# Two tiny transfers more, transposes moved between value rows, and some weight loads split or merged in a multimodal attention block

## The chip, the core and the metric

The kernel runs on one core of one Trainium2 chip. Its time is the device time of one execution in microseconds; the median of some executions stands for it. A profiled execution gives the trace: what each engine did and when, and when each transfer was issued and landed. TensorE (PE) multiplies and transposes, VectorE (DVE), ScalarE (ACT) and GpSimd (POOL) do the elementwise work, SyncE (SP) issues most transfers. Each engine takes its instructions in the order in which the program gives them.

## The reference

It is one attention block of a diffusion transformer with an image stream (2 batches of 256 tokens) and a text stream (2 batches of 32), D = 1152, all in bfloat16.

```
mod_i = silu(c) @ wmod_img          # six parts: shift, scale and gate are used
hi    = layernorm(x_img) * (1 + sci) + shi
qkvi  = hi @ wqkv_img               # the same for text, with its own weights
q, k, v = concat(text, image)
a     = softmax(q k^T / sqrt(D)) v
out_i = x_img + gai * (a_i @ wo_img)
out_t = x_txt + gat * (a_t @ wo_txt)
```

## The kernel before

The 512 image tokens are four tiles of 128 (tile 0 and 1 are batch 0, tile 2 and 3 batch 1). D is nine blocks of 128, `KT = 9`. The blocks are taken in four chunks `KC`: blocks 0-1, 2-3, 4-5 and 6-8. The order of the work is written out by hand: a manual schedule, in which each engine runs its instructions in the order of the source, and semaphores are put in where one engine needs another's result.

The change lies in the first stage, in which the image values are computed (`v = hi @ wqkv_img[:, 2D:]`) while the first weights still arrive. For each tile the stage does this:

- VectorE takes the statistics (`stats_of`), ScalarE the square root of the variance (`std_of`), VectorE writes the normalised rows `xn_i` (`out_of`).
- TensorE transposes `xn_i` block by block. The first two blocks are the heads (`x_heads`), the other seven the tails (`x_tails`). `head_scaled` scales the heads on ScalarE while it copies them into `hT_i`; `tail_out` copies the tails unscaled, on ScalarE for tiles 0 and 2, on VectorE for tile 1. Tails are scaled later in place (`apply_mod`), when the scale of their chunk is known.
- The scale comes from `w_sc_i`, which is loaded in four pieces. `mod_scale` multiplies it for chunks 0 to 2 (line 223), `mod_scale_last` for the last chunk (lines 240 and 245); VectorE turns that result into columns (line 248).
- The value products are the wide ones, 512 columns each, two per tile and block (`v_wide`, line 282; `v_row` is both of one block), and the narrow ones for the last 128 columns (`v_narrow`, line 294). They are summed over the nine blocks in banks of the accumulator: two banks per tile, and one for the narrow columns of all tiles. There are seven banks in the pool for these, and heads and tails of tiles 0 to 2 use the same pool in part, so a product may have to wait until an earlier tile's bank has been emptied.
- Tile 3 is transposed late (`last_transposes`, lines 306 and 309), when all its scales are known.

After that the shift of the modulation is added to `hT_i`, and the Q and K projections of the image follow (line 529), then the text stream, scores, softmax, attention and the output projections, which TensorE runs nearly without a gap.

Transfers: tiles 0 and 1 of x are issued by ScalarE, all else at the start by SyncE in the order of the source: scale pieces, x tiles and rows of the value weights `w_v_i` (one row is one block, 288 KB; rows 7 and 8 are one transfer, line 110), then the other weights in pieces (`load_w`, line 76; `K2` splits a weight into blocks 0-4 and 5-8). The transfers on these queues share eight completion counters in turn, so in the built program each transfer waits for the landing of the one that had its counter before.

Of the kernel before, what the change touches and what calls it, by code (L numbers as in the profile page):

```python
# [14 lines left out]
def kernel(  # L15
# [14 lines left out]
    nc = tc.nc  # L30
# [4 lines left out]
    B, NI, D = x_img.shape  # L35
    NT = x_txt.shape[1]
    P = 128
    KT = D // P
    NTOK = NI + NT
    NIT = (B * NI) // P  # L40
    TPB = NI // P
    NTT = B * NT
    CH = 384
    NCH = D // CH
    VC = 288
# [3 lines left out]
    KC = [(0, 2), (2, 4), (4, 6), (6, KT)]  # L49
# [9 lines left out]
    ps_sm = ctx.enter_context(tc.tile_pool(name="ps_sm", bufs=1, space=PSUM))  # L59
# [4 lines left out]
    xi_flat = x_img.rearrange("b n d -> (b n) d")  # L64
# [5 lines left out]
    def w_view(src):  # L70
        return src.rearrange("(kt p) n -> p kt n", p=P)

    def load_w(src, c0, ksplits=((0, KT),), home=None):
        t = wpool.tile([P, KT, D], bf, tag="w", name="t") if home is None else act.tile([P, KT, D], bf, tag=home, name="w_home")
        for (k0, k1) in ksplits:
            nc.sync.dma_start(t[:, k0:k1, :], w_view(src)[:, k0:k1, c0:c0 + D])
        return t
# [6 lines left out]
    xf_full = act.tile([P, 2 * VC + 64], bf)  # L84
    xf = xf_full[:, 0:2 * VC].rearrange("p (h j) -> p h j", h=2)
    w_sc_i = wpool.tile([P, KT, D], bf, tag="w", name="w_sc_i")
    w_v_i = act.tile([P, KT, D], bf, tag="V", name="w_v_i")

    def load_x(i, eng=nc.sync):
        eng.dma_start(x_i[:, i, :], xi_t[:, i, :])  # L90

    def load_sc(ch):
        k0, k1 = KC[ch]
        nc.sync.dma_start(w_sc_i[:, :, k0 * P:k1 * P], w_view(wmod_img)[:, :, D + k0 * P:D + k1 * P])

    def load_v(ch):
        for kt in range(*KC[ch]):
            nc.sync.dma_start(w_v_i[:, kt:kt + 1, :], w_view(wqkv_img)[:, kt:kt + 1, 2 * D:3 * D])  # L98

    for i in range(TPB):  # L100
        load_x(i, nc.scalar)
    load_sc(0)
    load_x(2)
    load_v(0)
    for ch in range(1, len(KC)):
        load_sc(ch)
        if ch < len(KC) - 1:
            load_v(ch)
    for k0, k1 in ((6, 7), (7, KT)):
        nc.sync.dma_start(w_v_i[:, k0:k1, :], w_view(wqkv_img)[:, k0:k1, 2 * D:3 * D])  # L110
        if k1 < KT:
            load_x(3)
    K3 = ((0, 3), (3, 6), (6, KT))
    K2 = ((0, 5), (5, KT))
# [50 lines left out]
    def ln_stats(x_ap, np_, k0=0, k1=NCH, stats=None):  # L165
        if stats is None:
            stats = small.tile([P, NCH, 6], f32, tag="stats")
        for k in range(k0, k1):
            nc.vector.bn_stats(stats[0:np_, k, :], x_ap[:, k * CH:(k + 1) * CH])  # L169
        return stats  # L170

    def ln_std(stats, np_):
        mv = small.tile([P, 2], f32, tag="mv")
        nc.vector.bn_aggr(mv[0:np_, :], stats[0:np_, :, :])
        rstd = small.tile([P, 1], f32, tag="rstd")
        nc.scalar.activation(rstd[0:np_, :], mv[0:np_, 1:2], ACT.Sqrt, bias=eps_t[0:np_, :])
        return mv, rstd

    def ln_apply(x_ap, np_, out_ap, mv, rstd, c0=0, c1=D):
        if c0 == 0:  # L180
            nc.vector.reciprocal(rstd[0:np_, :], rstd[0:np_, :])
        nc.vector.tensor_scalar(out_ap[:, c0:c1], x_ap[:, c0:c1], mv[0:np_, 0:1], rstd[0:np_, :],
                                op0=ALU.subtract, op1=ALU.mult)
# [10 lines left out]
    H = KC[0][1]  # L194
# [3 lines left out]
    def x_heads(i):  # L198
        pool, tag = (ps_sm, "sm") if i == 1 else (ps_mm, "mm")
        tp = pool.tile([P, H, P], bf, tag=tag, name="tph")  # L200
        for kt in range(H):
            nc.tensor.transpose(tp[:, kt, :], xn_i[:, i, kt * P:(kt + 1) * P], ident[:])
        return tp

    def head_scaled(tp, i):
        for kt in range(H):
            nc.scalar.activation(hT_i[:, kt, i * P:(i + 1) * P], tp[:, kt, :], ACT.Identity,
                                 scale=mod_i[:, kt, i // TPB:i // TPB + 1])

    def x_tails(i):  # L210
        pool, tag = (ps_mm, "mm") if i < TPB else (ps_sm, "sm")
        tp = pool.tile([P, KT - H, P], bf, tag=tag, name="tp")
        for kt in range(H, KT):
            nc.tensor.transpose(tp[:, kt - H, :], xn_i[:, i, kt * P:(kt + 1) * P], ident[:])
        return tp

    def tail_out(i, tp, k0, k1, on_vector=False):
        (nc.vector.tensor_copy if on_vector else nc.scalar.copy)(hT_i[:, k0:k1, i * P:(i + 1) * P], tp[:, k0 - H:k1 - H, :])
# [7 lines left out]
    def mod_scale(ch, eng, pool=ps_sm, tag="sm"):  # L226
        k0, k1 = KC[ch]
        mps = pool.tile([P, KT, B], f32, tag=tag)
        mod_cols(w_sc_i, mps, k0, k1)
        if eng == "dve":  # L230
            nc.vector.tensor_scalar_add(mod_i[:, k0:k1, :], mps[:, 0:k1 - k0, :], 1.0)
        else:
            nc.scalar.activation(mod_i[:, k0:k1, :], mps[:, 0:k1 - k0, :], ACT.Identity, bias=1.0)
# [43 lines left out]
    def v_wide(i, half, k0, k1, out=True):  # L277
        if k0 == 0:
            vacc[i, half] = ps_mm.tile([P, VW], f32, tag="mm", name=f"va{i}{half}")
        ps = vacc[i, half]  # L280
        for kt in range(k0, k1):
            nc.tensor.matmul(ps[:], lhsT=hT_i[:, kt, i * P:(i + 1) * P], rhs=w_v_i[:, kt, half * VW:(half + 1) * VW],  # L282
                             start=(kt == 0), stop=(kt == KT - 1))
        if k1 == KT and out:
            v_wide_out(i, half)

    def v_wide_out(i, half):
        evac(v_i[:, i, half * VW:(half + 1) * VW], vacc[i, half][:], "act" if i < TPB else None)

    def v_narrow(i, k0, k1):  # L290
        if i == 0 and k0 == 0:
            vacc["n"] = ps_mm.tile([P, NIT, P], f32, tag="mm", name="van")
        for kt in range(k0, k1):
            nc.tensor.matmul(vacc["n"][:, i, :], lhsT=hT_i[:, kt, i * P:(i + 1) * P], rhs=w_v_i[:, kt, NM:D],  # L294
                             start=(i == 0 and kt == 0), stop=(i == NIT - 1 and kt == KT - 1))

    def v_row(i, kt):
        v_wide(i, 0, kt, kt + 1)
        v_wide(i, 1, kt, kt + 1)

    def last_transposes(k0, k1, pool, tag):
        i = NIT - 1
        b = i // TPB
        tp = pool.tile([P, k1 - k0, P], bf, tag=tag, name="tp")
        for kt in range(k0, k1):
            nc.tensor.transpose(tp[:, kt - k0, :], xn_i[:, i, kt * P:(kt + 1) * P], ident[:])
        for j0 in range(k0, k1, 4):
            j1 = min(j0 + 4, k1)
            nc.vector.tensor_mul(hT_i[:, j0:j1, i * P:(i + 1) * P], tp[:, j0 - k0:j1 - k0, :],
                                 mod_i[:, j0:j1, b:b + 1].to_broadcast([P, j1 - j0, P]))  # L310
# [6 lines left out]
    def stats_of(i, k0, k1):  # L317
        lns[i] = ln_stats(x_i[:, i, :], P, k0, k1, lns.get(i))

    def std_of(i):  # L320
        lns[i] = ln_std(lns[i], P)

    def out_of(i, c0=0, c1=D):
        ln_apply(x_i[:, i, :], P, xn_i[:, i, :], *lns[i], c0, c1)
# [5 lines left out]
    out_of(0)  # L330
    mod_scale(0, "act")
    out_of(1)
    tails = []
    for i in range(TPB):
        heads = x_heads(i)
        tails.append(x_tails(i))
        head_scaled(heads, i)
    stats_of(2, 0, NCH)
    tail_out(0, tails[0], H, H + 3)
    std_of(2)  # L340
    tail_out(0, tails[0], H + 3, KT)
    tail_out(1, tails[1], H, H + 3, on_vector=True)
    out_of(2, 0, H * P)
    tail_out(1, tails[1], H + 3, KT, on_vector=True)
    out_of(2, H * P, D)
    for kt in range(*KC[0]):
        for i in range(TPB):
            v_row(i, kt)
    for i in range(TPB):
        v_narrow(i, *KC[0])  # L350
    head2 = x_heads(2)
    mod_scale(1, "dve")
    head_scaled(head2, 2)
    apply_mod(2, 0, 2, False, 0)
    apply_mod(3, 0, 2, False, 1)
# [16 lines left out]
    k0, k1 = KC[2]  # L372
# [14 lines left out]
    stats_of(3, 0, NCH)  # L387
    std_of(3)
    out_of(3)
    k0 = KC[3][0]  # L390
    for i in range(3):
        v_row(i, k0)
        v_narrow(i, k0, k0 + 1)
    for i in range(3):
        for half in range(2):
            v_wide(i, half, k0 + 1, KT)
        v_narrow(i, k0 + 1, KT)
        if i == 1:
            last_transposes(0, KT - 1, ps_sm, "sm")
            last_transposes(KT - 1, KT, ps_mm, "mm")  # L400
    v_wide(3, 0, 0, KT)
    v_narrow(3, 0, KT)
# [54 lines left out]

    w_k_i = load_w(wqkv_img, D, K3)
    w_sh_t = load_w(wmod_txt, 0)
    w_sc_t = load_w(wmod_txt, D, K2)  # L460
    nc.sync.dma_start(x_t[0:P:P // NTT, :], xt_flat[:, :])
    w_q_t = load_w(wqkv_txt, 0, K2)
    w_k_t = load_w(wqkv_txt, D, K2)
    w_ga_i = load_w(wmod_img, 2 * D, K2, home="V")
    w_v_t = load_w(wqkv_txt, 2 * D, K3)
    w_o_i = load_w(wo_img, 0, K2)
    w_ga_t = load_w(wmod_txt, 2 * D)
# [461 lines left out]
```

## Time and profile before

| | |
|---|---|
| median of three runs | 114.62 us (114.5 to 114.75) |
| the profiled execution | 114.88 us |
| its span in the trace | 113.1 us |
| granted TensorE clock, mean | 0.997 |
| PE busy in the span | 108.3 us (96%) |
| DVE, ACT, POOL busy | 76.1, 36.6, 28.4 us |
| bytes moved | 40.87 MB, mean 361 GB/s |

A row of the timeline has the start in us from the beginning of the span, the length, the engine, the line of the kernel, the operation, what it writes and reads, and how many instructions it merges; a bracket tells how long the engine was idle before and what ended that. A row of the transfers has the destination and the source, the issuing queue, the count, the size and the time from issue to landing. A row of the chain of waits has start, length and what ran or was waited for. Matmuls are pipelined: the length of one row is longer than the time by which it holds up the next, which is seen from start to start.

### The profile page before, as it was taken

How to read it: one execution, taken by the hardware profiler on the slowest of the kernel's cores; microseconds unless marked ns; L12 is line 12 of the kernel's file. 1: busy time of each engine (PE TensorE's matmuls, PEld its weight loads, DVE VectorE, ACT ScalarE, POOL GpSimd, SP SyncE). 2: the span in 40 equal slices, each digit the busy share in tenths (PEclk: the TensorE clock that was granted, in tenths of full speed). 3: DMA queues.
4: the chain of work that ended last, by engine and by line, in shares of the span. 5: the costliest groups of instructions: out<-in, count | busy, mean ns of one | idle time of the engine just before them, and what ended most of it. 6: DMA issues, size and time to landing. Idle time of an engine off the chain costs nothing.

```text
span 113.1 us, 2863 instructions
## 1 busy us (share of the span) xinstructions
PE 108.3 (96%) x1195; PEld 64.0 (57%) x1204; DVE 76.1 (67%) x151; ACT 36.6 (32%) x83; POOL 28.4 (25%) x65
## 2 busy tenths in 40 slices
PE   5999999999999999999999999999999999999990
PEld 1356655555444444444446558787687556567670
DVE  1699330956399999999999950237666802995971
ACT  4537500372190071740008924025646700001000
POOL 7100120730140000000000060601550470699300
PEclk9999999999999999999999999999999999999998
DMA  3999999999999999999999999999999999994052
GB/s 92 343 333 355 375 375 405 412 411 408 407 412 412 410 411 402 413 410 412 412 411 415 408 405 407 408 392 394 407 411 397 412 408 406 371 375 161 0 191 70
DMA packets 22839, 40.87 MB, mean 361 GB/s; under 512 B 1375, under 2 KB 6635, under 8 KB 22827
## 3 DMA queue, kind: packets, MB, share of 16 engines
q1 hardware_dynamic: 21547, 39.05, 90.4%
q10 hardware_dynamic: 672, 0.77, 2.2%
q0 software_dynamic: 608, 0.88, 2.1%
q8 instruction: 9, 0.15, 0.5%
q14 instruction: 3, 0.02, 0.1%
HBM read 39.36 MB, written 1.34 MB: 360 GB/s over the span
## 4 chain that ended last, share of the span: by engine, by line
PE 80%; DMA 13%; SPq 4%; issue 1%; DVE 0%
PE qkps L529 31%; PE ps L851 16%; DMA w_sc_i<-in_wmod_img_dram 13%; PE va L282 7%; PE aps L759 5%; PE ps L590 4%; PE sps L619 4%; PE gps L429 3%; SPq L98 3%; PE ops L869 2%; PE ps L694 2%; PE van L294 1%; PE gps L824 1%; PE sps L632 1%; PE pk L703 1%
## 5 line engine op out<-in xcount | busy, mean ns | idle before, releaser
L529 PE MATMUL qkps<-hT_i,t 128*128 128x512 bf16 x158 | 35.4, 379 | 0.2
L529 PEld LDWEIGHTS <-t 128*128 128x128 bf16 x162 | 15.6, 98 | 18.7 <-issue 0.4
L491 DVE SCALAR_TENSOR_TENSOR sacc<-w_v_i,mcols,sacc 128x1152 f32<-128x1152 bf16 x16 | 22.7, 1418 | 0.5
L282 PE MATMUL va<-w_v_i,hT_i 128*128 128x512 bf16 x67 | 17.0, 379 | 0.5 <-issue 0.3
L851 PE MATMUL ps<-t,aT 128*128 128x384 bf16 x99 | 16.4, 326 | 0.0
L851 PEld LDWEIGHTS <-aT 128*128 128x128 bf16 x117 | 11.0, 98 | 6.8 <-issue 0.5
L282 PEld LDWEIGHTS <-hT_i 128*128 128x128 bf16 x72 | 6.4, 98 | 6.2 <-issue 0.2
L835 POOL TENSOR_TENSOR w_og<-t,gb 128x384 bf16<-128x384 bf16 x9 | 8.7, 999 | 4.5 <-DMA gb<-mod_scratch 4.5
L857 DVE TENSOR_TENSOR tmp<-ps,gb 128x384 bf16<-128x384 f32 x11 | 6.0, 550 | 5.6 <-DMA gb<-mod_scratch 5.0
L548 POOL TENSOR_SCALAR mod_txt<-mcols 128x18 f32<-128x18 f32 x2 | 0.6, 275 | 32.4 <-DVE mcols L435 32.4
L169 DVE BATCH_NORM_STATS2 stats<-x_i 128x6 f32<-128x384 bf16 x12 | 5.8, 541 | 2.6 <-DMA x_i<-in_x_img_dram 2.6
L143 PE MATMUL wps<-wz 128*128 128x512 bf16 x15 | 6.1, 578 | 1.2 <-DVE wz L125 1.2
L479 ACT ACTIVATE qT<-qkps 128x512 bf16<-128x512 f32 x9 | 4.7, 600 | 6.9 <-PE qkps L529 6.9
L495 ACT CAST shi<-sacc 128x1152 bf16<-128x1152 f32 x2 | 2.3, 1154 | 13.2 <-DVE sacc L491 13.2
L772 DVE TENSOR_SCALAR aT<-aps,sv 128x288 bf16<-128x288 f32 (+2 forms) x11 | 4.3, 455 | 2.0 <-PE aps L759 2.0
L590 PEld LDWEIGHTS <-t 128*128 128x128 bf16 x162 | 5.0, 98 | 0.5
L157 DVE CAST kT<-qkps 128x512 bf16<-128x512 f32 x3 | 2.1, 686 | 4.7 <-PE qkps L529 4.7
L590 PE MATMUL ps<-hT_t,t 128*128 128x64 bf16 x162 | 5.0, 193 | 0.0
L858 DVE TENSOR_TENSOR o<-tmp,x_i 128x384 bf16<-128x384 bf16 x11 | 4.7, 426 | 0.4
L759 PE MATMUL aps<-pT,v_i 128*128 128x288 bf16 (+2 forms) x44 | 4.8, 264 | 0.0
L774 ACT ACTIVATE aT<-aps,sv 128x288 bf16<-128x288 f32 (+2 forms) x11 | 4.0, 468 | 2.1 <-PE aps L759 2.1
L619 PE MATMUL sps<-kT,qT 128*128 128x288 bf16 x36 | 4.6, 286 | 0.0
(160 smaller groups left out, 139.7 us busy)
## 6 DMA issues: line engine op xcount, KB each, us to landing
t<-in_wqkv_img_dram SPq DMA_DIRECT2D x6, 864.0 KB, 13.2
t<-in_wmod_txt_dram SPq DMA_DIRECT2D x2, 2592.0 KB, 17.6
t<-in_wqkv_txt_dram SPq DMA_DIRECT2D x2, 1440.0 KB, 14.2
t<-in_wmod_img_dram SPq DMA_DIRECT2D x3, 864.0 KB, 12.3
t<-in_wqkv_txt_dram SPq DMA_DIRECT2D x3, 864.0 KB, 14.1
t<-in_wo_txt_dram SPq DMA_DIRECT2D x3, 864.0 KB, 15.5
t<-in_wqkv_txt_dram SPq DMA_DIRECT2D x2, 1152.0 KB, 15.0
w_v_i<-in_wqkv_img_dram SPq DMA_DIRECT2D x7, 288.0 KB, 6.9
```

The source lines that it names most:

```text
L143: nc.tensor.matmul(ps[:], lhsT=wz[:, 0:P], rhs=wz[:], start=True, stop=True)
L169: nc.vector.bn_stats(stats[0:np_, k, :], x_ap[:, k * CH:(k + 1) * CH])
L282: nc.tensor.matmul(ps[:], lhsT=hT_i[:, kt, i * P:(i + 1) * P], rhs=w_v_i[:, kt, half * VW:(half + 1) * VW], start=(kt == 0), stop=(kt == K ...
L479: nc.scalar.mul(out_ap, in_ap, SCALE)
L491: nc.vector.scalar_tensor_tensor(saccs[b][:], w_v_i[:, kt, :], ap, saccs[b][:], op0=ALU.mult, op1=ALU.add)
L529: nc.tensor.matmul(pss[j - j0][:], lhsT=wq[:, kt, j * P:(j + 1) * P], rhs=hT_i[:, kt, :], start=(kt == 0), stop=(kt == KT - 1))
L590: nc.tensor.matmul(ps[:, j - j0, :], lhsT=wq[:, kt, j * P:(j + 1) * P], rhs=hT_t[:, kt, :], start=(kt == 0), stop=(kt == KT - 1))
L619: nc.tensor.matmul(sps[:], lhsT=qkTs[0][:, ft, b, q0:q0 + P], rhs=qkTs[1][:, ft, b, :], start=(ft == 0), stop=(ft == KT - 1))
L759: nc.tensor.matmul(bank[:, off:off + c1 - c0], lhsT=lhsT, rhs=rhs, start=(first[id(bank)] == n), stop=(final[id(bank)] == n))
L835: nc.gpsimd.tensor_mul(w_og[:, dt, 0:CH], w_o_i[:, dt, NG0:D], gb[:, B - 1, NG0:D])
L851: nc.tensor.matmul(ps[:, 0:cw], lhsT=aT[:, dt, t0:t0 + P], rhs=rhs, start=(dt == DTS[0]), stop=(dt == DTS[-1]))
L857: nc.vector.tensor_mul(tmp[:, 0:cw], ps[:, 0:cw], gb[:, b, cs])
```

## The change

- ScalarE issues two more transfers behind tiles 0 and 1 of x: 16 rows of two elements (4 bytes) each, one from x, one from the first block of the value weights, into columns of `xf_full` that nothing reads.
- Rows 7 and 8 of the value weights are a transfer each. Three later weights (`w_sc_t`, `w_q_t`, `w_ga_i`) are one transfer each instead of two.
- The heads of tiles 0 and 1 are both transposed first, and ScalarE scales them block by block in turn. The tails of tile 0 are transposed behind the first value row of tile 0, those of tile 1 behind the four first rows. The copies of the tails come later on ScalarE and VectorE: tile 0's behind the square root of tile 2, tile 1's behind the normalisation of tile 2, which is now one instruction instead of two.
- The heads of tile 2 are transposed ahead of the narrow products of chunk 0.
- In the last chunk the products go block by block: row 6 for tiles 0 to 2, row 7 for tiles 0 and 1, then row 8 of tile 0, row 8 of tile 1, and rows 7 and 8 of tile 2. The first eight transposes of tile 3 stand behind tile 0 instead of tile 1.

```diff
     for i in range(TPB):
         load_x(i, nc.scalar)
+    nc.scalar.dma_start(xf_full[0:16, 2 * VC + 2:2 * VC + 4], xi_flat[2 * P:4 * P:16, 0:2])
+    nc.scalar.dma_start(xf_full[0:16, 2 * VC:2 * VC + 2], wqkv_img[0:P:8, 2 * D:2 * D + 2])
...
-    for k0, k1 in ((6, 7), (7, KT)):
-        nc.sync.dma_start(w_v_i[:, k0:k1, :], w_view(wqkv_img)[:, k0:k1, 2 * D:3 * D])
-        if k1 < KT:
+    for kt in range(*KC[-1]):
+        nc.sync.dma_start(w_v_i[:, kt:kt + 1, :], w_view(wqkv_img)[:, kt:kt + 1, 2 * D:3 * D])
+        if kt == KC[-1][0]:
             load_x(3)
...
-    def head_scaled(tp, i):
-        for kt in range(H):
+    def head_scaled(tp, i, k0=0, k1=H):
+        for kt in range(k0, k1):
...
-    tails = []
+    heads = [x_heads(i) for i in range(TPB)]
+    for kt in range(H):
+        for i in range(TPB):
+            head_scaled(heads[i], i, kt, kt + 1)
+    stats_of(2, 0, NCH)
+    v_row(0, 0)
+    tails = [x_tails(0)]
+    std_of(2)
+    tail_out(0, tails[0], H, H + 3)
+    tail_out(0, tails[0], H + 3, KT)
+    out_of(2)
+    v_row(1, 0)
     for i in range(TPB):
-        heads = x_heads(i)
-        tails.append(x_tails(i))
-        head_scaled(heads, i)
-    stats_of(2, 0, NCH)
-    tail_out(0, tails[0], H, H + 3)
-    std_of(2)
-    tail_out(0, tails[0], H + 3, KT)
+        v_row(i, 1)
+    tails.append(x_tails(1))
     tail_out(1, tails[1], H, H + 3, on_vector=True)
-    out_of(2, 0, H * P)
     tail_out(1, tails[1], H + 3, KT, on_vector=True)
-    out_of(2, H * P, D)
-    for kt in range(*KC[0]):
-        for i in range(TPB):
-            v_row(i, kt)
+    head2 = x_heads(2)
     for i in range(TPB):
         v_narrow(i, *KC[0])
-    head2 = x_heads(2)
     mod_scale(1, "dve")
...
-    k0 = KC[3][0]
     for i in range(3):
-        v_row(i, k0)
-        v_narrow(i, k0, k0 + 1)
+        v_row(i, KT - 3)
+        v_narrow(i, KT - 3, KT - 2)
+    for i in range(TPB):
+        v_row(i, KT - 2)
+        v_narrow(i, KT - 2, KT - 1)
     for i in range(3):
+        k0 = KT - 1 if i < TPB else KT - 2
         for half in range(2):
-            v_wide(i, half, k0 + 1, KT)
-        v_narrow(i, k0 + 1, KT)
+            v_wide(i, half, k0, KT)
+        v_narrow(i, k0, KT)
+        if i == 0:
+            last_transposes(0, KT - 1, ps_sm, "sm")
         if i == 1:
-            last_transposes(0, KT - 1, ps_sm, "sm")
             last_transposes(KT - 1, KT, ps_mm, "mm")
...
-    w_sc_t = load_w(wmod_txt, D, K2)
+    w_sc_t = load_w(wmod_txt, D)
...
-    w_q_t = load_w(wqkv_txt, 0, K2)
+    w_q_t = load_w(wqkv_txt, 0)
...
-    w_ga_i = load_w(wmod_img, 2 * D, K2, home="V")
+    w_ga_i = load_w(wmod_img, 2 * D, home="V")
```

## The prediction

> **What bounds the kernel now.** I read the chain of waits first, then the timeline of the first 32 us engine by engine, then the transfers. The built program of the changed kernel gave the new order and the waits of each queue, without times.
>
> ```profile
> PE 80%; DMA 13%; SPq 4%; issue 1%; DVE 0%
> 1.21 5.34 DMA w_sc_i<-in_wmod_img_dram
> ...
> 10.29 8.84 DMA w_sc_i<-in_wmod_img_dram
> ...
> 19.18 0.57 PE sps L245 x36
> ...
> 31.35 10.03 PE qkps L529 x46
> 31.30:89.00 57.70, 57.49 (x686) 34.29 (x688) 45.03 (x74) 23.30 (x54) 8.81 (x21) 1.00 1.04 407
> ```
>
> The first lines are the chain: until 19.14 (10.29 + 8.84) it hangs on the pieces of the scale weights `w_sc_i`; from 19.18 on it is TensorE, which the whole chain names for 80%. The last line is a window (length, busy time of TensorE, its weight loads, VectorE, ScalarE, GpSimd, then granted clock, share of the transfer engines, GB/s): from 31.3 to 89 TensorE is busy 57.49 of 57.70 us. So whatever shifts the start of the Q projection (`qkps`, near 31.3) shifts the end by as much, unless a weight is late. All edits to the order lie before 31.3; I work out where TensorE stands there.
>
> **Heads, tails and tile 2 (7.8 to 19.2 us).** Before:
>
> ```profile
> 7.90 0.58 DVE L182 TENSOR_SCALAR xn_i<-x_i,mv,rstd 128x1152 bf16<-128x1152 bf16 x1
> 8.24 1.25 ACT L207 ACTIVATE hT_i<-tph,mod_img 128x128 bf16<-128x128 bf16 x4 [0.22 <-PE tph L202]
> 8.66 0.55 PE L214 MATMUL tp<-ident,xn_i 128*128 128x128 bf16 x7
> 9.05 1.89 PE L282 MATMUL va<-w_v_i,hT_i 128*128 128x512 bf16 x7
> 10.37 0.57 ACT L218 COPY hT_i<-tp 128x512 bf16<-128x512 bf16 x1
> 10.70 0.34 DVE L182 TENSOR_SCALAR xn_i<-x_i,mv,rstd 128x256 bf16<-128x256 bf16 x1
> 10.77 0.39 PE L294 MATMUL van<-w_v_i,hT_i 128*128 128x128 bf16 x4
> 11.10 0.29 PE L202 MATMUL tph<-ident,xn_i 128*128 128x128 bf16 x2
> 11.23 0.59 PE L223 MATMUL mps<-sT,w_sc_i 128*128 128x2 bf16 x18
> 11.43 0.63 ACT L207 ACTIVATE hT_i<-tph,mod_img 128x128 bf16<-128x128 bf16 x2 [0.49 <-PE tph L202]
> ...
> 12.33 0.28 PE L294 MATMUL van<-w_v_i,hT_i 128*128 128x128 bf16 x2
> ...
> 18.89 0.23 PE L240 MATMUL sps<-ones_full 128*32 128x96 bf16 x4
> ```
>
> A transpose takes 0.056 us of TensorE (seven from 8.66 to 9.05), a wide value product 0.216 (eight from 9.05 to 10.77, one unrecorded), a narrow one 0.056. Before, tile 0's tails filled the time in which VectorE still normalised tile 1 (until 7.90 + 0.58); now that time is idle. Tile 1's two heads end at 8.66 as before, and the first value row starts there: of the four head scalings in 1.25 us from 8.24, the first ends near 8.6. Four rows and 14 tails: 8.66 + 8 x 0.216 + 14 x 0.056 = 11.17. ScalarE scales the heads in the order in which the rows want them, one in 0.3 us, and stays ahead; the interleaving itself costs nothing.
>
> Tile 2's heads come next. Before, only 256 columns of tile 2 were normalised for them (10.70, 0.34 us). Now the whole tile is, 0.58 by the row at 7.90: ready at 11.28, heads at 11.335 instead of 11.10. The four narrow products moved behind them use, in the built program, the bank of tile 0's tails; ScalarE now empties it behind tile 2's square root, in 0.4 and 0.57 us from 10.37, until about 11.35. They start at 11.46: no wait. The scale products, begun at 11.68 instead of 11.23, are through at 12.13. Then tile 2's first wide product: in the built program it waits for both of tile 2's head scalings, since its bank is the one those read; before, it waited for one. The scalings follow the heads by 0.33: 11.66 to 12.29. So the product starts at 12.34 and the narrow ones at 12.77, against 12.33: TensorE is 0.44 late. DVE's tail copies of tile 1, now behind the normalisation, follow from 11.3; the rows that read them come after 13.
>
> TensorE is dense from 12.33 to 18.89, so the 0.44 arrives there. L245 could have started near 18.96 and waited for the weights until 19.18: 0.22 of slack. It now starts at about 19.39: **+0.21**. If the bank wait and the late heads were not there it would be 0 (lower bound); both terms in full with no slack, 0.44.
>
> **The last value rows (20.4 to 31.3 us).**
>
> ```profile
> 13.58 0.43 SPq L110 DMA_DIRECT2D w_v_i<-in_wqkv_img_dram  x1
> w_v_i<-in_wqkv_img_dram SPq DMA_DIRECT2D x1, 576.0 KB, 8.4
> 20.11 0.68 DVE L262 TENSOR_SCALAR hT_i<-hT_i,scols 128x256 bf16<-128x256 bf16 x2
> 20.70 1.47 DVE L169 BATCH_NORM_STATS2 stats<-x_i 128x6 f32<-128x384 bf16 x3
> ...
> 21.87 0.22 PE L294 MATMUL van<-w_v_i,hT_i 128*128 128x128 bf16 x1
> 22.05 1.02 PE L282 MATMUL va<-w_v_i,hT_i 128*128 128x512 bf16 x4
> 23.00 0.58 DVE L182 TENSOR_SCALAR xn_i<-x_i,mv,rstd 128x1152 bf16<-128x1152 bf16 x1
> ...
> 24.50 1.03 PE L282 MATMUL va<-w_v_i,hT_i 128*128 128x512 bf16 x4
> ```
>
> The two last weight rows came as one transfer, landing at 13.58 + 8.4 = 21.98. The narrow product at 21.87 leaves TensorE free at 21.92, and the next starts at 22.05: a wait of 0.12. With rows of their own, row 7 should land near 21.3, and row 8 at 21.98 is first read 0.98 later. **-0.12.** But eight transposes of tile 3 now stand behind row 8 of tile 0 instead of tile 1. From 21.92: two tiles of row 7 and one of row 8, each 2 x 0.216 + 0.056 = 0.488, end at 23.39. Tile 3's normalised rows are ready at 23.58 (23.00 + 0.58) and TensorE gets them at 23.63: **+0.25**. Before, tile 1's products stood in front too and the nine transposes, ending at 24.50, began at 24.00, so the wait was hidden. VectorE's way to that tile begins with the scale columns that L245 makes (20.11) and goes on without a gap (20.70), so it moves with the 0.21 and saves none of it. In full: 23.63 + 8 x 0.056 + 0.488 + 0.056 = 24.63, against 24.50: +0.13, plus 0.21: **+0.34** at tile 2's last rows. VectorE scales tile 3 from about 24.5, over a microsecond ahead of use. From there the order is unchanged, and the Q projection begins 0.34 later.
>
> **Transfers.**
>
> ```profile
> 0.74 0.87 ACTq L90 DMA_DIRECT2D x_i<-in_x_img_dram  x2
> ...
> 3.47 1.28 ACT L176 ACT_TABLE_LOAD   x1
> 5.58 0.29 ACT L176 ACTIVATE rstd<-mv,eps_t 128x1 f32<-128x1 f32 x1 [0.83 <-DVE mv L174]
> 2.39 0.91 SPq L98 DMA_DIRECT2D w_v_i<-in_wqkv_img_dram  x2
> w_v_i<-in_wqkv_img_dram SPq DMA_DIRECT2D x1, 288.0 KB, 6.0
> w_v_i<-in_wqkv_img_dram SPq DMA_DIRECT2D x1, 288.0 KB, 6.2
> 3.82 2.49 SPq L98 DMA_DIRECT2D w_v_i<-in_wqkv_img_dram  x2
> 3.80 1.48 DVE L169 BATCH_NORM_STATS2 stats<-x_i 128x6 f32<-128x384 bf16 x3 [2.64 <-DMA x_i<-in_x_img_dram]
> GB/s 92 343 333 355 375 375 405 412 411 408 407 412 412 410 411 402 413 410 412 412 411 415 408 405 407 408 392 394 407 411 397 412 408 406 371 375 161 0 191 70
> out_dram<-o SPq DMA_DIRECT2D x1, 32.0 KB, 1.5
> 87.08 2.12 SPq L76 DMA_DIRECT2D t<-in_wo_txt_dram  x1
> t<-in_wo_txt_dram SPq DMA_DIRECT2D x1, 864.0 KB, 15.4
> 101.98 2.38 PE L869 MATMUL ops<-t,aT 128*32 128x288 bf16 x72
> ```
>
> The two small issues take ScalarE about 0.87, as the two x issues did. Behind them stand two table loads, the second ending at 3.47 + 1.28 = 4.75; the first square root waits for VectorE until 5.58. Even moved by the whole 0.87 it is 0.04 late: nothing, at most that. On the transfer engines 32 rows more are a fifth of a percent of some 22,800 packets; bound, 0.1 us of the stream, and TensorE would not be waiting for it.
>
> The eight completion counters go round, so two more transfers change what SyncE waits for: value row 1 now waits for tile 0 of x (landed by 3.80, issued before in the second half of the row at 2.39), row 2 for the first scale piece (1.21 + 5.34 = 6.55, issued before at 3.82). Queued by then are 2.66 MB (three x tiles and two value rows of 288 KB, two scale pieces of 576 KB); at 92 GB/s in the first slice of 2.8 us and some 343 in the next two they last until 9.8, so row 2 comes three microseconds before the engines are idle. I take 0. Bound: they run dry for a microsecond.
>
> Merging three late weight loads moves no byte. Their readers' first products must now wait for whole loads; the 0.21 us that TensorE idles from 31.3 to 89 show that no half came late, but not by how much each was early (bound: a microsecond). The last weight of all lands at 87.08 + 15.4 = 102.5, and the last third of its reader's 2.38 us begins near 103.5. I take nothing, with that microsecond of cover.
>
> Two rows of 288 KB, issued some 0.46 us apart, land some 0.66 apart (6.0 and 6.2 after issue): one behind the other at the stream's rate, with no fixed time between them. So I take row 8 to land where the pair did. The Trainium skill, "DMA: Bandwidth & Descriptors", speaks against splitting a load: section Bandwidth asks for transfers of a megabyte or more, and the section on the anatomy of one DMA gives each about 2 us fixed, for GpSimd's path. Paid in series that would put row 8 near 24.0 and make the sum about +1.0 by that page, an estimate; the trace disagrees, with its 0.66.
>
> **Sum.** -0.12 + 0.25 + 0.21 = +0.34 us. The profiled execution took 114.88 (span 113.1, 1.78 around it); the median is 114.62. So 115.22 by the profiled one, **114.96** as a median, +0.3%. About 0.2% (0.23 us) is what a measurement can tell from no change.
>
> **Rivals.**
> - One of the two new waits isn't there: tile 3 is normalised by the time TensorE asks (decides at 23.6), or tile 2's lateness stays under the 0.22 of slack (decides at 18.96). Then +0.09 to +0.13: 114.73. If neither is, only the 0.12 is left: 114.50. For it: both are sums of small steps. Against: each is a dependence on rows above. Not slower by the measure. Chance 0.2.
> - The start gets quicker: with SyncE held back, the x tiles and scale pieces land sooner. To be faster by 0.23 or more, both VectorE's chain from 3.80 and the piece at 19.14 must come some 0.5 us sooner: 114.3. Against: the first five transfers are issued as before. Chance 0.08.
> - The held queue runs the engines dry, and the scale piece lands a microsecond later, at 20.1 instead of 19.14. TensorE, there at 19.39, would lose 0.75 more: 115.7. Chance 0.1.
> - A fixed time per transfer, paid in series. The smallest store, 32 KB, takes 1.5 us to land. Row 8 would land at 23.5, where TensorE wants it at 23.11 (22.90 + 0.21): 0.4 later, of which 0.25 falls into the wait for tile 3: +0.5 in all, 115.1. Against: the 0.66 above. Chance 0.04. [...]
>
> **Numbers.** The forecast has 0.58. Low: the first rival's upper cases, 114.7; high: forecast with half of a dry microsecond, 115.5. Left out are the faster case, most of the dry one and a few hundredths at either side: just under 0.2. Slower 0.7, same 0.21, faster 0.09.
>
> **What would show it.** Tile 2's heads near 11.33, its first wide product near 12.34, L245 near 19.39 with no wait for a transfer, no gap before row 7, a gap of about 0.25 before the transposes of tile 3 that VectorE ends, and the Q projection near 31.6. It is wrong if L245 still waits for its weights, if tile 3's transposes run on without a gap, or if TensorE waits for a transfer that it does not wait for now.

## The result, and the profile after

| | median us | runs | profiled execution (span) |
|---|---|---|---|
| before | 114.66 (114.50 to 114.79) | 6 | 114.88 (113.1) |
| after | 115.14 (114.94 to 115.21) | 6 | 115.13 (113.3) |

The ratio is 1.0040, with a 95% interval of 1.0027 to 1.0053: 0.46 us slower (0.31 to 0.61), where 0.34 was forecast. The two profiled executions differ by 0.25.

The chain of waits of the kernel after, by engine, and one window (length, busy time of TensorE, its weight loads, VectorE, ScalarE, GpSimd, then clock, DMA share, GB/s):

```profile
PE 86%; DVE 7%; DMA 3%; ACT 1%; issue 0%
31.57:89.30 57.73, 57.73 (x690) 34.31 (x688) 45.02 (x74) 23.31 (x54) 8.81 (x21) 1.00 1.04 408
```

Before, 13% of the chain were transfers, nearly all of it the scale weights that the strip waited for. That link is gone: the strip is late for another reason, and the chain goes back through VectorE to the x tiles. From the Q projection on, 57.73 us of work take 57.73 (before: 57.49 of 57.70): no merged weight load is late.

The timeline of the kernel after (start, length in us, engine, line, operation; in this stage the line numbers are two higher than in the kernel before):

```profile
11.28 0.28 PE L204 MATMUL tph<-ident,xn_i 128*128 128x128 bf16 x2
11.40 0.39 PE L296 MATMUL van<-w_v_i,hT_i 128*128 128x128 bf16 x4
11.60 0.63 ACT L209 ACTIVATE hT_i<-tph,mod_img 128x128 bf16<-128x128 bf16 x2 [0.34 <-PE tph L204]
11.62 0.59 PE L225 MATMUL mps<-sT,w_sc_i 128*128 128x2 bf16 x18
12.28 0.59 PE L284 MATMUL va<-w_v_i,hT_i 128*128 128x512 bf16 x2
...
19.27 0.23 PE L242 MATMUL sps<-ones_full 128*32 128x96 bf16 x4
19.32 0.56 PE L247 MATMUL sps<-w_sc_i,sT 128*32 128x96 bf16 x36
...
22.01 0.22 PE L296 MATMUL van<-w_v_i,hT_i 128*128 128x128 bf16 x1
22.07 0.59 PE L284 MATMUL va<-w_v_i,hT_i 128*128 128x512 bf16 x2
...
23.14 0.58 DVE L184 TENSOR_SCALAR xn_i<-x_i,mv,rstd 128x1152 bf16<-128x1152 bf16 x1
23.48 0.22 PE L296 MATMUL van<-w_v_i,hT_i 128*128 128x128 bf16 x1
23.78 0.62 PE L308 MATMUL tp<-ident,xn_i 128*128 128x128 bf16 x8
```

Three places answer to the three terms of the sum. The strip (L247) follows its ones products (L242) after 0.05, so it waits for no transfer; before it started at 19.18, so it is 0.14 late. Row 7 (the wide products at 22.07) follows the narrow product of 22.01 without the former wait of 0.12. And the transposes of tile 3 start 0.30 after the last narrow product, where 0.056 is normal: 0.25 of wait, ended by VectorE's normalisation (23.14 + 0.58 = 23.72). 0.14 - 0.12 + 0.25 = 0.27; the Q projection starts at 31.57 instead of 31.29, and the last store is issued 0.26 later.

### The profile page after: what moved, and what is told of

It reads as the page before. It is cut to its first block, busy times and chain, and to the rows that moved or that the text cites. A ratio compares the mean times of both kernels' runs of the same rounds, so it can differ in the third digit from the quotient of the medians.

```text
span 113.3 us, 2870 instructions
## 1 busy us (share of the span) xinstructions
PE 108.1 (95%) x1204; PEld 63.6 (56%) x1204; DVE 75.6 (67%) x150; ACT 36.8 (32%) x83; POOL 28.5 (25%) x65
## 4 chain that ended last, share of the span: by engine, by line
PE 86%; DVE 7%; DMA 3%; ACT 1%; issue 0%
PE qkps L536 31%; PE ps L858 16%; PE va L284 11%; PE aps L766 5%; PE ps L597 4%; PE sps L626 4%; DVE stats L171 4%; PE gps L436 3%; DMA x_i<-in_x_img_dram 3%; PE ops L876 2%; PE ps L701 2%; DVE xn_i L184 2%; PE gps L831 1%; PE tp L216 1%; PE sps L639 1%; PE van L296 1%
## 5 line engine op out<-in xcount | busy, mean ns | idle before, releaser
L284 PE MATMUL va<-w_v_i,hT_i 128*128 128x512 bf16 x72 | 17.7, 379 | 0.1
L145 PE MATMUL wps<-wz 128*128 128x512 bf16 x15 | 5.2, 503 | 1.2 <-DVE wz L127 1.2
```

Of the source, the lines that this page charges most:

```text
L145: nc.tensor.matmul(ps[:], lhsT=wz[:, 0:P], rhs=wz[:], start=True, stop=True)
```

## The experiments

Each ran beside the kernel before on the same chip (29 runs in each of three sets; its medians were 114.69, 114.72 and 114.70). Differences in us below are (ratio - 1) x 114.7. Most are known to 0.15 to 0.25 us only, so two of them can be told apart when they lie some 0.3 us apart; where less is at stake, the traces decide. "Before" as a base means that the edit is made to the kernel before.

### The change in three parts

**Last value rows alone** (before, with the split of rows 7 and 8, their products row by row, and tile 3's first transposes behind tile 0):

```diff
-    for k0, k1 in ((6, 7), (7, KT)):
+    for kt in range(*KC[-1]):
...
-        v_row(i, k0)
-        v_narrow(i, k0, k0 + 1)
+        v_row(i, KT - 3)
+        v_narrow(i, KT - 3, KT - 2)
+    for i in range(TPB):
+        v_row(i, KT - 2)
+        v_narrow(i, KT - 2, KT - 1)
```

> The kernel before with the last value rows of the change alone (rows 7 and 8 a transfer each, products row by row, tile 3's first eight transposes behind tile 0). Theory of waits: the 0.12 us in front of row 7 goes and TensorE waits about 0.25 before tile 3's transposes; the Q projection begins 0.13 later, so +0.13 us (0.05 to 0.2). Rival, the transfers at the start and SyncE's waits cost the time: no new wait matters here, -0.12 to 0. Rival, the change only shifts the run as a whole by chance: 0.

Measured: 115.77, ratio 1.0088 (1.0064 to 1.0111): +1.0, a miss by 0.9. TensorE alone doesn't hold it: its Q projection starts at 31.70, 0.41 later than before, and every later product keeps that distance to the end. Of the 0.41, 0.27 stand at the strip already (19.45, in an execution with a late second x tile, on which more at the end), and 0.13 come behind it, as forecast. The rest, about a microsecond, lies behind the last store. It is taken up below.

**Heads, tails and tile 2 alone:**

```diff
-        heads = x_heads(i)
-        tails.append(x_tails(i))
-        head_scaled(heads, i)
+    heads = [x_heads(i) for i in range(TPB)]
+    for kt in range(H):
+        for i in range(TPB):
+            head_scaled(heads[i], i, kt, kt + 1)
...
+    v_row(0, 0)
+    tails = [x_tails(0)]
```

> The kernel before with the new order of heads, tails and tile 2 alone. Theory of waits: tile 2's first wide product starts near 12.34 and its narrow ones near 12.77 (12.33 before), the strip of scale products near 19.39 without a wait for its weights, and nothing later waits: +0.21 us (0.1 to 0.3). If the bank of tile 2's heads were not awaited: 0 to 0.05, because the 0.22 us of slack before the strip takes it up. Rival, the transfers cost the time: 0.

Measured: 114.98, ratio 1.0016 (1.0004 to 1.0028): +0.18. The number is as expected, the trace is not:

```profile
19.29 0.56 PE L245 MATMUL sps<-w_sc_i,sT 128*32 128x96 bf16 x36
...
21.98 0.22 PE L294 MATMUL van<-w_v_i,hT_i 128*128 128x128 bf16 x1
22.03 1.03 PE L282 MATMUL va<-w_v_i,hT_i 128*128 128x512 bf16 x4
```

The strip is 0.11 late and waits for no transfer, but the Q projection starts at 31.28, as in the trace of before (31.29). Rows 7 and 8 still come as one transfer here, and TensorE now reaches row 7 so late that it has landed (21.98): the wait of 0.12 in front of it takes up what the strip lost. By the forecast's own rows 0.21 - 0.12 = +0.09 was to be expected of this kernel, not +0.21; that the median shows 0.18 is not explained by these two traces.

**Transfers alone** (the two small ones and the three merges):

```diff
+    nc.scalar.dma_start(xf_full[0:16, 2 * VC + 2:2 * VC + 4], xi_flat[2 * P:4 * P:16, 0:2])
+    nc.scalar.dma_start(xf_full[0:16, 2 * VC:2 * VC + 2], wqkv_img[0:P:8, 2 * D:2 * D + 2])
...
-    w_sc_t = load_w(wmod_txt, D, K2)
+    w_sc_t = load_w(wmod_txt, D)
```

> The kernel before with the two small transfers and the three merged loads alone; rows 7 and 8 stay one transfer, the order of the work is that of before. Theory of waits: SyncE holds value row 1 until about 3.7 and row 2 until about 6.6, the engines do not run dry, the last scale piece lands within 0.1 of 19.13, and the time is that of before: 0 (-0.1 to 0.1). Rival, the transfers cost the time: +0.3 to +0.5, with a TensorE wait for a transfer that grew.

Measured: 114.74, ratio 0.9995 (0.9979 to 1.0010): nothing, as expected. SyncE held rows 1 and 2 until 3.79 and 6.47, but the last scale piece landed at 18.57 where 19.13 was expected, and TensorE came to the strip later than that, because the second x tile was late in this execution too.

### The two new waits, taken away one by one

**Tile 3's first transposes behind tile 1 again** (in the kernel after):

```diff
-        if i == 0:
-            last_transposes(0, KT - 1, ps_sm, "sm")
         if i == 1:
+            last_transposes(0, KT - 1, ps_sm, "sm")
```

> The changed kernel with tile 3's first eight transposes put back behind tile 1. Theory of waits: the gap of 0.25 us before them goes, for TensorE reaches them 0.49 later; against before there remains +0.21 - 0.12 = +0.09 us in the trace, 0.25 less than the changed kernel. Rival, the transfers cost the time: as the changed kernel, +0.48.

Measured: 114.98, ratio 1.0024 (1.0006 to 1.0042): +0.28, 0.18 less than after where 0.25 was expected; the medians alone could not tell that from nothing. The trace can: the gap in front of the transposes is gone, and from the strip to the Q projection TensorE takes 11.99 us instead of 12.25.

**Narrow products of the first rows ahead of tile 2's heads** (in the kernel after):

```diff
+    for i in range(TPB):
+        v_narrow(i, *KC[0])
     head2 = x_heads(2)
-    for i in range(TPB):
-        v_narrow(i, *KC[0])
```

> The changed kernel with the four narrow products of the first rows put back ahead of tile 2's heads, so that tile 2's first wide product waits for its own head scaling alone; tile 2 is still normalised whole. By the forecast's sum the late strip (+0.21) goes for the greater part, the wait for tile 3 (0.25) stays or grows by what TensorE comes sooner: 0 to 0.2 below the changed kernel, 114.95 to 115.15, with the strip near 19.2. If the wait for tile 3 absorbs it (TensorE sooner, tile 3 not): no change. Rival (the order of heads and tails costs nothing): no change, strip at 19.3.

Measured: 115.03, ratio 1.0028 (1.0011 to 1.0044): +0.32, 0.14 less than after. Its timeline:

```profile
10.70 0.58 DVE L184 TENSOR_SCALAR xn_i<-x_i,mv,rstd 128x1152 bf16<-128x1152 bf16 x1
11.18 0.39 PE L296 MATMUL van<-w_v_i,hT_i 128*128 128x128 bf16 x4
11.40 0.28 PE L204 MATMUL tph<-ident,xn_i 128*128 128x128 bf16 x2
11.52 0.59 PE L225 MATMUL mps<-sT,w_sc_i 128*128 128x2 bf16 x18
12.19 0.30 PEld L284 LDWEIGHTS <-hT_i 128*128 128x128 bf16 x2 [0.17 <-ACT hT_i L209]
12.22 0.59 PE L284 MATMUL va<-w_v_i,hT_i 128*128 128x512 bf16 x2
...
19.26 0.56 PE L247 MATMUL sps<-w_sc_i,sT 128*32 128x96 bf16 x36
```

The first wide product of tile 2 now waits for one head scaling, and still starts only 0.06 earlier (12.22 against 12.28), as the strip does (19.26 against 19.32). The edit changes two things at once: one scaling is awaited instead of two, but tile 2's heads now stand behind the four narrow products and come at 11.40 instead of 11.28, and their scalings with them. The one gives back most of what the other saves, so this run doesn't price the second scaling by itself. Nor is it the whole-tile normalisation that holds these heads (it ends at 11.28): TensorE is late already. The narrow products start at 11.18 (10.77 before), because the seven transposes of tile 0's tails, 0.39 us, no longer fill the idle time while tile 1 is normalised.

**Both at once:**

> The changed kernel with both new waits taken away: narrow products of the first rows ahead of tile 2's heads, and the first eight transposes of tile 3 behind tile 1. If the two waits are all that the change costs: before - 0.12 to before + 0.1, 114.6 to 114.8. If heads and tails cost otherwise (the interleaved scalings, the idle time while tile 1 is normalised): 114.9 or more.

Measured: 114.78, ratio 1.0012 (1.0000 to 1.0024): +0.14. Its timeline:

```profile
19.29 0.56 PE L247 MATMUL sps<-w_sc_i,sT 128*32 128x96 bf16 x36
...
21.98 0.22 PE L296 MATMUL van<-w_v_i,hT_i 128*128 128x128 bf16 x1
22.04 0.59 PE L284 MATMUL va<-w_v_i,hT_i 128*128 128x512 bf16 x2
...
23.93 0.22 PE L296 MATMUL van<-w_v_i,hT_i 128*128 128x128 bf16 x1
23.99 0.67 PE L308 MATMUL tp<-ident,xn_i 128*128 128x128 bf16 x9
```

The strip is 0.11 late, row 7 has no wait (-0.12), the transposes follow the narrow product by 0.06 and start where they did before (23.99). Its Q projection starts at 31.28, as in before. Of the 0.46 the two edits thus take away 0.32 (some 0.2 either way), and the traces say which: the Q projection starts 0.29 earlier than in after, the strip only 0.03, so nearly all of it is the wait for tile 3. The 0.14 left (0 to 0.28) is hardly what a measurement can tell, and its trace doesn't show it.

### The end of the program

Why did the last rows alone cost 0.9 too much? The split makes one transfer more, and the eight completion counters go round: the last store came on the first counter instead of the eighth. At the end SyncE waits for the counters one after another, always from the first to the eighth. Its wait record and its drains at the end (count, min/median/max ns, first to last start), in the kernel with the last rows alone:

```profile
SPq L928 <- DMA out_dram<-o: 1.1, 1, 1.1
L928 SPq DRAIN  x3: 7/13/110, 113.1 to 114.0; - x3
```

**Last rows with one merge**, so that the number of transfers is that of before:

```diff
-    w_sc_t = load_w(wmod_txt, D, K2)
+    w_sc_t = load_w(wmod_txt, D)
```

> As the kernel with only the last value rows changed, with one merge added (w_sc_t in one transfer), so that the number of transfers is again that of the kernel before and the last store falls on the eighth of the eight completion counters. Theory A (SyncE walks the counters in a fixed order at the end of the program; the kernel with only the last value rows had one transfer more, so its last store fell on the first counter and seven waits stood behind it): the 0.9 us between its last landing and its end go, 114.8, which is before + 0.13 by the two waits of TensorE. Rival B (the split or the order of the rows itself costs a microsecond somewhere): 115.7 as without the merge.

Measured: 114.88, ratio 1.0016 (1.0000 to 1.0031): +0.18. The extra time at the end is gone, as the theory of the counters says, and the rest (0 to 0.36) agrees with the two waits of TensorE (+0.13).

```profile
SPq L928 <- DMA out_dram<-o: 0.6, 2, 0.4
L928 SPq DRAIN  x3: 7/7/13, 112.6 to 113.2; - x3
```

Here SyncE has gone through the first counters by the time the last store lands; with the last store on the first counter it waits there 1.1 in one piece and then walks the others.

**Before with one small transfer more**, nothing else:

```diff
+    nc.scalar.dma_start(xf_full[0:16, 2 * VC + 0:2 * VC + 2], xi_flat[2 * P:4 * P:16, 0:2])
```

> The kernel before with one more transfer of 16 rows of 4 bytes behind the x tiles, into columns that nobody reads, nothing else. Last store on the first counter. Theory A: seven waits of about 0.063 us behind the last landing, 0.45, and the 0.4 by which SyncE's last drain came later there: 115.1 with the waits alone, 115.6 with both. Rival B (counters don't matter): 114.7.

Measured: 115.05, ratio 1.0040 (1.0023 to 1.0058): +0.46, for 64 bytes.

```profile
SPq L925 <- DMA out_dram<-o: 1.1, 1, 1.1
L925 SPq DRAIN  x3: 7/7/7, 112.7 to 113.3; - x3
```

**After without the two small transfers:**

> The changed kernel without the two transfers of 16 rows of 4 bytes. The last store falls on the sixth of the eight counters, so two of SyncE's waits stand behind its landing: +0.13 by 0.063 each; SyncE is held less at the start, which the stream doesn't show as long as it doesn't run dry: 115.15 to 115.3 (the changed kernel: 115.14). Rival (the held queue costs time with two transfers as it does with four, where it cost 1.4): some 0.3 sooner, 114.85.

Measured: 115.27, ratio 1.0062 (1.0041 to 1.0084): +0.71, 0.25 more than after (0.13 by the medians), which agrees with the two later counters, and no sooner for a freer queue. In the trace the Q projection starts at 31.57 as in after, the last store lands at 112.43 (112.42), and what is longer is the end.

From the records of the last landing and of SyncE's waits and drains in the traces, in us:

| kernel | counter of the last store | last store lands | first drain after it | end of the span after it |
|---|---|---|---|---|
| before | 8th | 112.16 | 0.09 | 0.94 |
| after | 8th | 112.42 | 0.08 | 0.93 |
| last rows, one merge | 8th | 112.50 | 0.09 | 0.96 |
| transfers alone | 7th | 112.23 | 0.14 | 0.99 |
| after, no small ones | 6th | 112.43 | 0.20 | 1.05 |
| four more | 4th | 113.64 | 0.37 | 1.24 |
| one more | 1st | 112.12 | 0.56 | 1.42 |
| last rows alone | 1st | 112.57 | 0.56 | 1.91 |

Each counter behind that of the last store costs 0.05 to 0.07 us: (0.56 - 0.09) / 7 = 0.067. In the kernel with the last rows alone this is 0.47 of the 0.97 by which its end is longer; the other 0.5 stands between SyncE's drains (113.1 to 114.0, where the others need 0.3 to 0.6). Why they are late there and not with one more transfer, I could not settle.

In the change two small transfers, one for the split and minus three for the merges make zero: the last store stays on the eighth counter. So the pieces are not worth what each costs alone: without the split's +1 the transfers alone land on the seventh, and the split alone on the first.

### The held queue

**Before with four small transfers more:**

> The kernel before with four such transfers. Last store on the fourth counter. Theory A: four waits of 0.063 us behind the last landing, 0.25, with or without the late drain of 0.4: 114.95 or 115.35. A theory in which each small transfer costs a fixed time: four times what one costs. Rival B: 114.7.

Measured: 116.59, ratio 1.0173 (1.0135 to 1.0211): +1.98 (1.87 by the medians; one of its six runs took 117.84, at a granted clock of 0.983), far beyond the counters' 0.25. SyncE's issue of rows 0 and 1 and the strip, in its timeline, and two windows of it:

```profile
3.76 3.07 SPq L98 DMA_DIRECT2D w_v_i<-in_wqkv_img_dram  x2
...
20.62 0.57 PE L249 MATMUL sps<-w_sc_i,sT 128*32 128x96 bf16 x36 [0.60 <-DMA w_sc_i<-in_wmod_img_dram]
6.90:8.10 1.20, 0.45 (x19) 0.35 (x15) 1.14 (x4) 0.01 (x1) 0.00 (x0) 1.00 0.67 138
8.00:12.00 4.00, 3.24 (x30) 2.01 (x31) 3.70 (x13) 2.74 (x9) 0.00 (x0) 1.00 1.03 293
```

SyncE's issue of value rows 0 to 3 in the kernel after and its two windows:

```profile
2.46 1.61 SPq L98 DMA_DIRECT2D w_v_i<-in_wqkv_img_dram  x2
6.70 0.80 SPq L98 DMA_DIRECT2D w_v_i<-in_wqkv_img_dram  x2
6.90:8.10 1.20, 0.71 (x20) 0.45 (x16) 1.12 (x5) 0.41 (x2) 0.00 (x0) 1.00 1.04 384
8.00:12.00 4.00, 3.60 (x47) 2.40 (x46) 3.47 (x9) 2.80 (x9) 0.00 (x0) 1.00 1.07 346
```

The two windows of the kernel before:

```profile
6.90:8.10 1.20, 1.16 (x26) 0.85 (x24) 1.11 (x5) 0.47 (x2) 0.00 (x0) 1.00 1.01 321
8.00:12.00 4.00, 3.91 (x50) 2.58 (x49) 3.72 (x11) 2.97 (x10) 0.00 (x0) 1.00 1.07 350
```

In the kernel after, value row 0 goes out at 2.46 and row 1 once tile 0 of x has landed; the windows carry 384 and 346 GB/s (before: 321 and 350). With four small transfers it is row 0 that is held until 3.76 and row 1 until 6.50 (before: 2.39 and 2.86), with all that stands behind them in the queue. Between 6.9 and 8.1 us the transfer engines then run short of work: their share is 0.67 and the stream 138 GB/s. From 8 to 12 they are busy again but move less, 293; why, the trace doesn't show. TensorE is 0.90 late itself from the first transposes on (8.75 against 7.85), mostly because the second x tile landed at 6.28 in this run; on top of that it waits 0.60 for the scale piece, whose landing sets the strip at 20.62, 1.44 later than before. This is the mechanism of the prediction's third rival, at more than its price; with two small transfers it doesn't set in. One profiled execution shows it. In the four others with a late second x tile the stream stays at 334 GB/s or more from 8 to 12.

### Two tries to beat both kernels

**Before with the split, transposes behind tile 1 as before, one merge:**

> The kernel before with the last value rows in transfers of their own and row by row, the first eight transposes of tile 3 behind tile 1 as before, and w_sc_t merged, so that the last store stays on the eighth counter. By the forecast's -0.12 alone: 114.6, Q projection at 31.17 with the strip at 19.18. Rival (the scaled columns of the last strip are next late, as in the kernel with the narrow products moved): no change, 114.7.

Measured: 114.63, ratio 1.0002 (0.9988 to 1.0017). In its trace the wait before row 7 is gone and the transposes follow without a gap:

```profile
21.82 0.22 PE L294 MATMUL van<-w_v_i,hT_i 128*128 128x128 bf16 x1
21.87 0.59 PE L282 MATMUL va<-w_v_i,hT_i 128*128 128x512 bf16 x2
...
23.77 0.22 PE L294 MATMUL van<-w_v_i,hT_i 128*128 128x128 bf16 x1
23.82 0.67 PE L306 MATMUL tp<-ident,xn_i 128*128 128x128 bf16 x9
```

The Q projection starts 0.17 earlier than in the trace of before, 0.12 of it by the wait; but the ratio shows no gain, and 0.12 is less than the measurement can tell.

**The same with four narrow products moved ahead of the strip:**

```diff
+    for i in range(TPB):
+        v_narrow(i, k0, k1)
     mod_scale_last()
```

> A candidate to beat both kernels: the kernel before with the last value rows in transfers of their own and row by row, the first eight transposes of tile 3 behind tile 1 again, the four narrow products of rows 4 and 5 for tiles 0 and 1 moved ahead of the last scale strip, and w_sc_t merged so that the number of transfers stays. By the waits of TensorE: no wait before row 7, -0.12, four narrow products of 0.056 in the 0.22 of idle time ahead of the strip, -0.22: 114.35 at best, 114.55 if only one of them works. Rival B (the split costs): above 115.

Measured: 114.74, ratio 1.0003 (0.9990 to 1.0016): nothing.

```profile
18.96 0.23 PE L240 MATMUL sps<-ones_full 128*32 128x96 bf16 x4
19.33 0.57 PE L245 MATMUL sps<-w_sc_i,sT 128*32 128x96 bf16 x36
20.27 0.28 PE L294 MATMUL van<-w_v_i,hT_i 128*128 128x128 bf16 x2
20.60 0.11 PEld L282 LDWEIGHTS <-hT_i 128*128 128x128 bf16 x2 [0.23 <-DVE hT_i L262]
```

The four narrow products had covered the way from the strip over VectorE to the first scaled row. Taken from there, they leave 0.23 of new wait before that row: the idle time only changed its place, since the scale piece's landing holds the strip and the strip holds the row.

## Why the prediction was right, step by step

- **The bound** held: the Q projection's shift (0.28) is the shift of the last store (0.26).
- **Heads, tails, tile 2 (+0.21 forecast).** Heads at 11.28 (forecast 11.335), first wide product 12.28 (12.34), strip 19.32 (19.39) without waiting for a transfer: +0.14. All three steps are 0.06 early, as is tile 0 of x, landed at 3.72 instead of 3.77. In this trace both waits are there as forecast: the heads follow the whole-tile normalisation, and tile 2's first product the second head scaling (12.23). What each is worth alone was not measured, since the kernel with the narrow products first moves the heads too.
- **The wait before row 7 (-0.12)** went, by the rows at 22.01 and 22.07. Rows 7 and 8 landed at 21.13 and 21.82 (forecast 21.3 and 21.98). But the forecast gave this gain to the split, and the kernel with heads and tails alone loses the same wait without it: its strip of 19.29 brings TensorE to row 7 when the pair has landed. The sum is right all the same, since it counts the wait once. (Two slips are without effect: row 8 is read 0.92 behind its landing, not 0.98, and 32 of 22,839 packets are 0.14%, not a fifth of a percent.)
- **The wait for tile 3 (+0.25)** is there with 0.25, and is ended by VectorE. It is the best shown of the terms: from the strip to the Q projection TensorE takes 12.25 us in all five kernels with tile 3's first transposes behind tile 0, and 11.99 in the six with them behind tile 1 and no wait before row 7; before, with that wait, it is 12.11.
- **Transfers (0)** are 0 by the kernel that has them alone. Rows 7 and 8 landed 0.69 apart, and splitting them costs nothing where the counters and tile 3's transposes stay (1.0002). The Trainium skill's "DMA: Bandwidth & Descriptors", in its section on the anatomy of one DMA, puts the fixed 2 us of a transfer on GpSimd's path mostly down to its completion. No run here measures that path; for a store of 32 KB that SyncE issues, the last one, the trace of after has it otherwise: of 1.46 us to its landing (110.96 to 112.42), 0.86 pass before its first packet and 0.34 behind its last. Rows in flight show no such times between them.
- **What the prediction didn't see** is the end of the program. It counted the counters only where SyncE issues loads. Its price of 0 for the transfers is right because +2, +1 and -3 cancel; had one merge been left out, the same reasoning would have been wrong by 0.5 us or more.
- **The size.** By traces the change costs 0.28 (forecast 0.34), by medians 0.46 (0.34). The base is part of it: the profiled execution of before was 0.22 above its median, that of after was at it. A single pair of traces fixes the strip's term no better: with heads and tails as before, the strip started between 19.05 and 19.45 in seven traces, with those of after between 19.26 and 19.51 in six (leaving out the kernel with four more). Most of that spread is the second x tile. Where it landed by 4.9, the strip started between 19.05 and 19.18 with the order of before (19.33 in the kernel with the four narrow products moved ahead) and between 19.26 and 19.32 with that of after; where it landed at 5.5 or later, between 19.37 and 19.45 against 19.51 in a single trace. So where the tile was in time the new order makes the strip 0.1 to 0.3 late; for the other case one trace is little. What the other 0.2 of the medians is, no trace shows. It isn't in the middle of the program: from the Q projection to the issue of the last store before and after take 79.40 and 79.39. The kernel with one transfer more, which has the order of before, started its Q projection at 31.12, so the trace of before may have been a late one.

## What to carry to other kernels

A term taken from one wait in one profiled execution (here 0.22 of slack behind a transfer) is a sample: the strip's start moved by 0.4 between runs with the same order of work, more than the term itself, so such a sum is worth a range of that width. When a change adds, splits or merges transfers, count them to the end of the program too: if completion counters go round, the counter on which the last store falls decides how many waits follow it. And filling an idle stretch with later work pays only if that work wasn't covering another wait.

## What the runs showed of the hardware that I had not expected

- SyncE's end-of-program wait costs 0.05 to 0.07 us for each counter behind the last store's, up to 0.47 for seven.
- The second x tile, issued at 1.15 in all traces, landed at 4.2 to 4.9 in nine of the 14 and at 5.5 to 6.3 in five. Where it is late, VectorE waits for it and tile 0's heads come later; where it isn't, and the order is that of before, the strip waits for its weights. The two cases, the first in the kernel with the transfers alone (VectorE's row, then TensorE's), the second in that with one more:

```profile
5.83 1.48 DVE L171 BATCH_NORM_STATS2 stats<-x_i 128x6 f32<-128x384 bf16 x3 [0.29 <-DMA x_i<-in_x_img_dram]
19.33 0.23 PE L242 MATMUL sps<-ones_full 128*32 128x96 bf16 x4
19.38 0.56 PE L247 MATMUL sps<-w_sc_i,sT 128*32 128x96 bf16 x36
```

```profile
19.05 0.57 PE L246 MATMUL sps<-w_sc_i,sT 128*32 128x96 bf16 x36 [0.22 <-DMA w_sc_i<-in_wmod_img_dram]
```

  In the first TensorE comes too late to wait for the piece, in the second it waits.
- Holding SyncE's queue at the very start (value rows 0 and 1 by 1.4 and 3.6 us, with all behind them) went with a stream of 138 instead of 321 GB/s between 6.9 and 8.1 us and of 293 instead of 350 between 8 and 12, in one execution.
